# A fused attention, gating and mixing block on one core: where the first raw weights are loaded, and in what order batch 0's v projection uses them

## The chip, the cores and the metric

The kernel runs on one NeuronCore of one Trainium2 chip. The metric is the device time of one execution, in microseconds (us). Three runs of the kernel before took 501.28, 501.58 and 502.6 us; their median is 501.58 us.

The engines are named as in the profile: PE is TensorE (matmuls; PEld its weight loads), DVE VectorE, ACT ScalarE, POOL GpSimd, SP SyncE. SP, ACT and POOL also issue DMAs; SPq, ACTq and POOLq are these issues. Each engine runs its instructions in one fixed order, so an instruction that waits holds up all that stand behind it on that engine.

## The reference

Four batches of 576 tokens pass through three blocks. In outline:

```python
# attention: 8 heads of 64; heads 0-3 see the last 32 tokens, heads 4-7 every 32nd token
scores = q @ k.T / 8, masked;  attn = softmax(scores);  x = attn @ v          # x: 4 x 576 x 512
# gating block
h = relu(x @ w_in)                       # w_in 512 x 1024
u, v = h[..., :512], h[..., 512:]
v_n = (v - mean(v)) / sqrt(var(v) + 1e-6)
x = (u * (w_spatial @ v_n + b)) @ w_out
# mixing block
theta = x @ w_theta
y = w_tok_r @ (x * cos(theta)) + w_tok_i @ (x * sin(theta))
u = x + y;  out = u + relu(u @ w_ch)
```

Most weights arrive as 64-bit floats. The kernel loads their raw words and converts them on the chip into two 16-bit parts, "hi" and "lo"; a product is then three matmuls (hi by hi, lo by hi, hi by lo).

## The kernel before

`attention0` is batch 0's attention. It runs in steps s = 0 to 10 over eight groups of blocks (`quads0`): step s issues the scores of group s, the transposed outputs of group s-3, the transposed probabilities of group s-1 and the products with v of group s-2. While it runs, every engine keeps the order of the program (`pinned`). The dictionary `aside` hangs further work on the steps: the functions in the first list run in the middle of a step, those in the second at its end.

That further work is the input weight `w_in`. `win_piece(half, i, by)` gives five functions for one row block (128 rows by 512 columns) of one half: `[0]` the DMA of the raw words (512 KB), `[1:3]` two ACT passes over them, `[3]` a DVE pass that joins the two results, and `[4]` the split into the hi part (ACT) and the lo part (POOL). The half for v is `wv`, the half for u is `wu`; four row blocks each, numbered 0 to 3. The raw words of row blocks 0 and 1 lie in the buffer that the trace calls `x2f`, those of 2 and 3 in `zf`; the joined 32-bit numbers lie in `x2h`, the finished weights in `win`. `wu[i]` uses the same place as `wv[i]`, so its load waits until `wv[i][3]` has read the raw words. Later weights use the same two buffers: `w_spT` is loaded into `x2f` and `zf` next.

`main_v(0)` is batch 0's v projection, a generator that `go` moves on by one yield. It has five token tiles: pairs `pr` = 0 and 1 of two tiles of 128 tokens each, and a tail of 64 tokens. `v_mm(ps, tile, c)` adds the row block c of the weight to one tile with three matmuls of 512 columns. `v_relu` (ACT) empties a pair into `vr` and DVE takes mean and variance of it (BATCH_NORM_STATS2, then AGGREGATE); `norm` then makes `vn`. `main_mid(0)` goes on with `u_chunk(0..3)`, which need all four `wu`, and `sp_chunk(0..3)`, which need `vn` and `w_spT`. Both take their PSUM tile from a pool of three (`pm`) that the scores of batch 1 (`attention1`, tiles `a`) and the v projection use too.

After `attention0` the order is no longer pinned: `pinned.clear()` hands it to a scheduler, which works from the order of the program, from the time at which TensorE should be by its own count (`clock`), and from the list `conv` of due times of the remaining weights. In the traces of this kernel nearly every instruction has the line L107, that of the helper that issues it, so rows are told apart by their tiles.

Of the kernel before, what the change touches and what calls it, by code (L numbers as in the profile page):

```python
# [33 lines left out]
N32 = 3  # L34
# [23 lines left out]
PREP_AT = (112.0, 126.0, 131.0)  # L58
# [11 lines left out]
def kernel(  # L70
# [52 lines left out]
    nc = Engines  # L123
# [19 lines left out]
    NC = DM // P  # L143
# [76 lines left out]
    def s1(name):  # L220
        return scr.tile([P, S], F32, tag="s1", name=name, bufs=3)

    def pm(name):
        return ps_m.tile([P, 2, 512], F32, tag="pm", name=name)
# [67 lines left out]
    def win_piece(half, i, by):  # L292


        r = slice(i % 2 * DM, i % 2 * DM + DM)
        stg, x = (raw0, raw1)[i // 2][:, r], vals[i // 2][:, r]
        c = slice(half * DM, (half + 1) * DM)
        steps = from_f64(stg, x, DM)
        return [lambda: by.dma_start(stg, w_in[i * P:(i + 1) * P, c])] + steps + [
            lambda: part(win[:, 0, i:i + 1, c], win[:, 1, i:i + 1, c], x.unsqueeze(1), False)]  # L300
# [181 lines left out]
    def load_vs(b, v, hps, blocks=range(11), by=None):  # L482

        by = by or nc.sync
        src = vs_d[b].rearrange("h p n j d -> p h n (j d)")
        c = slice(1, VW - 1) if b == 0 else slice(0, P)
        hs = slice(hps[0] - 2, hps[-1] - 1)
        for i in blocks:
            k, end = CB * i, min(CB * i + CB, S)
            o = 0  # L490
            while k < end:
                n = max(range(5), key=lambda n: (SOFF[n] <= k) * (min(SOFF[n] + P, end) * 8 - n))
                m = min(end, SOFF[n] + P) - k
                p0 = k - SOFF[n]
                r = 64 * (i % 2) + o
                by.dma_start(v[r:r + m, :, i // 2, c], src[p0:p0 + m, hs, n])
                k += m
                o += m
# [29 lines left out]
    def load_mask16():  # L528
        mf = s1("mf")[:, 0:4 * P].rearrange("p (n c) -> p n c", n=4)
        nc.sync.dma_start(mf, mask_d)  # L530
        nc.gpsimd.tensor_copy(mask, mf)
# [114 lines left out]
    def attention0(aside):  # L646

        xf = xT[1].rearrange("p e c n -> p (e c n)").bitcast(F32)  # L650
        vf = wtok.rearrange("p e i n -> p (e i n)").bitcast(F32)
        qk = kts + [xf[:, i * 2 * S:(i + 1) * 2 * S].rearrange("p (j n) -> p j n", j=2) for i in range(2)]
        q, k = [t[:, 0] for t in qk], [t[:, 1] for t in qk]
        v01 = vf[:, 0:18 * VW].rearrange("p (h n d) -> p h n d", h=2, n=9)
        v23 = vf[:, 18 * VW:30 * VW].rearrange("p (h n d) -> p h n d", h=2, n=6)
        v = [v01[:, i] for i in range(2)] + [v23[:, i] for i in range(2)]
        S0, S1 = 2 * QB, 7 * CB + QB
        for hp in range(2):
            load_q(0, hp, q[hp], 0, S0, nc.sync)
            load_k(0, hp, k[hp], 0, S0, nc.scalar)  # L660
        for hp in (2, 3):
            load_qk(0, hp, q[hp], k[hp], 0, S1)
        nc.scalar.activation(x2f[:, 0, 0:1], halfpi, AF.Exp)
        for hp in (2, 3):
            load_k(0, hp, k[hp], S1, S, nc.scalar)
        make_masks()
        bias = bias_load()
        for n in range(2):
            nc.gpsimd.memset(v01[:, n, 0:9, 0:VW:VW - 1], 1.0)
            nc.gpsimd.memset(v23[:, n, 0:6, 0:VW:VW - 1], 1.0)  # L670
        load_vs(0, v23, (2, 3), range(8), nc.gpsimd)
        for f in aside[-1][:2]:
            f()
        load_vs(0, v23, (2, 3), range(8, 11), nc.gpsimd)
        for f in aside[-1][2:]:
            f()
        load_vl(0, v01, (0, 1), range(3))
        for hp in (2, 3):
            load_q(0, hp, q[hp], S1, S, nc.sync)
        for hp in range(2):  # L680
            load_qk(0, hp, q[hp], k[hp], S0, S)
        load_vl(0, v01, (0, 1), range(3, 4))
        load_mask16()
        un = {}
        for s in range(NG + 3):
            mid, end = aside.get(s, ((), ()))
            if s < NG:
                sc = pm("a0")
                t = s2("smx")
                sm, pT = t[:, 0, 0:512], t[:, 1, 0:512].rearrange("p (n k) -> p n k", n=4)  # L690
                st = att_p.tile([P, 2, 8], F32, tag="st", name="st", bufs=4)
                un[s] = sm, pT, st
                qd_scores(quads0[s], q, k, sc)
                qd_shift(quads0[s], sc, sm, st)
            if s >= 3:
                sm, pT, st = un.pop(s - 3)
                local = quads0[s - 3][0]
                qd_out(0, quads0[s - 3], pT, pm("xt")[:, 0, :] if local or s == 6 else pa("sc"))
            if 1 <= s <= NG:
                sm, pT, st = un[s - 1]  # L700
                qd_turn(quads0[s - 1], sm, pa4("av"), pT)
            if s < NG:
                qd_exp(quads0[s], un[s][0])
            if s == 1:
                bias_part(bias)
            for f in mid:
                f()
            if 2 <= s < NG + 2:
                sm, pT, st = un[s - 2]
                local = quads0[s - 2][0]  # L710
                qd_pv(quads0[s - 2], v, pT, pa("sc").unsqueeze(1) if local else pm("pv"), st, pT)
            for f in end:
                f()
# [277 lines left out]
    def main_v(b):  # L991
# [4 lines left out]
        def v_relu(pr, ps):  # L996
            v = vr[pr] = s2(f"vr{pr}")
            if pr == 2:
                fold_tail(v[0:TL, 0, 0:DM], v[0:TL, 1, 0:DM], ps[:, 0, :])
                ha.activation(v[0:TL, 0, 0:DM], v[0:TL, 0, 0:DM], AF.Relu, scale=1.0 / PS)  # L1000
                rows, nt = TL, 1
            else:
                ha.activation(v[:, :, 0:DM], ps, AF.Relu, scale=1.0 / PS)
                rows, nt = P, 2
            bs = att_p.tile([P, 2, 6], F32, tag="bs", name="bs")
            for t in range(nt):
                hv.bn_stats(bs[0:rows, t, :], v[0:rows, t, 0:DM])
                hv.bn_aggr(mv[0:rows, 2 * pr + t, :], bs[0:rows, t, :])
# [26 lines left out]
        def v_mm(ps, i, c):  # L1035
            for n, (xe, we) in enumerate(PASS):
                clock[0] += DM
                marks.append((clock[0] / 2400.0, nc.tensor.matmul(
                    ps, xh[:, xe, c, i * P:(i + 1) * P], win[:, we, c, DM:2 * DM],
                    start=(c == 0 and n == 0), stop=(c == NC - 1 and n == 2)).ins.name))  # L1040

        if b == 0:
            for pr in range(2):
                ps = pm(f"v{pr}")
                for ts, cs in (((range(2), (0, 1)), (range(2), (2, 3))), ((range(1), range(NC)), (range(1, 2), range(NC))))[pr]:
                    for c in cs:
                        for t in ts:
                            v_mm(ps[:, t, :], 2 * pr + t, c)
                    yield
                v_relu(pr, ps)  # L1050
                if pr == 0:
                    yield
            norm((0, 1))
        for pr in V_ORDER if b else V_ORDER[2:]:
            ps = pm(f"v{pr}")
# [174 lines left out]
    conv = []  # L1230
# [18 lines left out]
    timed(sq_parts(wch, w_ch, 2), *CONV_CH)  # L1249
    atts = [None] + [attention1(b) for b in range(1, N32)] + [attention(b) for b in range(N32, B)]  # L1250
    for at, f in [(at, lambda n=n: tok_load(*toks[n])) for n, at in enumerate(TOK_AT)] + [
            (at, lambda: next(atts[N32])) for at in PREP_AT]:
        i = next((i for i, c in enumerate(conv) if c[0] > at), len(conv))
        conv.insert(i, (at, f))
    att = {"b": 1, "n": 0}
# [26 lines left out]
    wt = pa("av")  # L1282
    for _ in range(WARM):
        nc.tensor.matmul(wt[:, 0:P], ident, ident, start=True, stop=True)
    wv, wu = ([win_piece(half, i, by) for i in range(NC)] for half, by in ((1, nc.gpsimd), (0, nc.sync)))
    v0 = main_v(0)

    def go():
# [1 line left out]

    attention0({
        -1: [w[0] for w in wv],
        3: ((), wv[0][1:3]),
        4: ((), wv[0][3:4] + wv[1][1:3] + wu[0][:1]),
        5: ((), wv[0][4:] + wv[1][3:4] + wv[2][1:3] + wu[1][:1]),
        6: ((), wv[1][4:] + wv[2][3:4] + wv[3][1:3] + wu[2][:1]),
        7: ((), wv[2][4:] + wv[3][3:4] + wu[3][:1] + [go, step]),
        8: ((), wv[3][4:] + wu[0][1:3] + [go]),
        9: ([go], wu[0][3:4] + wu[1][1:3] + [go]),
        10: ((), wu[0][4:] + wu[1][3:4] + wu[2][1:3] + [go]),  # L1300
    })
    conv[:0] = [(0.0, f) for f in wu[1][4:] + wu[2][3:] + wu[3][1:]]
    pinned.clear()
    run_main(v0)
    for b in range(B):
# [92 lines left out]
```

## Time and profile before

| | before |
|---|---|
| median of three runs | 501.58 us |
| the profiled execution | 499.96 us |
| its span on the core | 498.2 us |
| PE busy | 470.7 us (94%) |
| DVE busy | 301.5 us (61%) |
| ACT busy | 269.5 us (54%) |
| POOL busy | 83.1 us (17%) |

The span is the time between the first and the last instruction of the profiled execution; 1.76 us of the execution lie around it. PE is busy nearly all the time after the first 120 us, so what other engines do there matters only where PE waits for them. In the first 120 us PE does wait, and the profile has to be read stage by stage: which engine or transfer ends the wait. A row of the timeline gives start, duration, engine, operation, the tile written and the tiles read, and in brackets the idle time of that engine before it and what ended it.

### The profile page before, as it was taken

The numbers are of one execution on the slowest core, as the hardware profiler recorded it, in microseconds if no ns is written. First come the engines' busy times: TensorE is split into PE (matmuls) and PEld (weight loads), VectorE is DVE, ScalarE is ACT, GpSimd is POOL, SyncE is SP. The second block draws the span as 40 slices with busy tenths as digits, with TensorE's granted clock in tenths as the row PEclk, the third lists the DMA queues.
The fourth block names the chain that finished last, engine by engine and source line by source line (L and its number), as shares of the span: only waits on it lengthen the run. The fifth ranks groups of instructions, "written<-read, shape, count | busy, mean of one in ns | idle before, by whom it ended". The sixth has DMA issues, their size and how long they took to land. (4 is left out here: it accounts for less than half of the span.)

```text
span 498.2 us, 10844 instructions
## 1 busy us (share of the span) xinstructions
PE 470.7 (94%) x4446; PEld 352.6 (71%) x4446; DVE 301.5 (61%) x653; ACT 269.5 (54%) x488; POOL 83.1 (17%) x86
## 2 busy tenths in 40 slices
PE   7578789889999999999999999999999999999996
PEld 5354466667667777777658777777657777777775
DVE  3465799886798744763488677872588121217412
ACT  3347678878984433545763767764862022148302
POOL 9313304320001500111001310021004200210220
PEclk9999999999999999999999999999999999999999
DMA  7937766664891035210174155321170020004502
GB/s 175 280 99 202 191 225 201 214 221 135 210 216 37 2 130 180 68 44 2 25 172 150 23 138 170 76 43 22 31 160 2 1 95 1 1 2 67 125 0 97
DMA packets 72250, 52.73 MB, mean 106 GB/s; under 512 B 51198, under 2 KB 61008, under 8 KB 72200
## 3 DMA queue, kind: packets, MB, share of 16 engines
q1 hardware_dynamic: 70248, 49.03, 36.5%
q0 software_dynamic: 1312, 2.70, 2.0%
q8 instruction: 35, 0.57, 0.5%
q10 hardware_dynamic: 640, 0.30, 0.3%
q14 instruction: 15, 0.12, 0.1%
HBM read 35.36 MB, written 4.72 MB: 80 GB/s over the span
## 5 line engine op out<-in xcount | busy, mean ns | idle before, releaser
L107 PE MATMUL y<-wtok,zf 128*128 128x288 f16 x864 | 107.2, 286 | 0.0
L107 PEld LDWEIGHTS <-zf 128*128 128x128 f16 x864 | 84.1, 98 | 22.2 <-issue 1.2
L107 PE MATMUL u<-xT,win 128*128 128x288 f16 x384 | 49.3, 286 | 2.3 <-ACT u L107 2.0
L107 PE MATMUL sp<-wsp,vn 128*128 128x288 f16 x384 | 50.5, 286 | 0.0
L107 POOL TENSOR_TENSOR x2h<-x2f,x2h 128x576 f16<-128x576 f32 x19 | 26.2, 1384 | 142.2 <-issue 66.7
L107 PE MATMUL x<-zf,wout 128*128 128x288 f16 x384 | 49.6, 286 | 0.0
L107 PE MATMUL v<-win,xT 128*128 128x512 f16 (+1 forms) x240 | 48.3, 380 | 0.0
L107 PE MATMUL th<-x2h,wth 128*128 128x288 f16 x384 | 47.7, 286 | 0.0
L107 PEld LDWEIGHTS <-vn 128*128 128x128 f16 x416 | 40.3, 98 | 10.2 <-DVE vn L107 0.5
L107 PEld LDWEIGHTS <-win 128*128 128x128 f16 x384 | 37.3, 98 | 11.8 <-issue 2.7
L107 PE MATMUL c<-x2h,wch 128*128 128x288 f16 x360 | 45.2, 286 | 0.0
L107 PEld LDWEIGHTS <-wth 128*128 128x128 f16 x384 | 37.6, 98 | 9.5
L107 PEld LDWEIGHTS <-wch 128*128 128x128 f16 x384 | 37.4, 98 | 9.2
L107 PEld LDWEIGHTS <-wout 128*128 128x128 f16 x384 | 36.8, 98 | 9.5
L107 PEld LDWEIGHTS <-xT 128*128 128x128 f16 (+1 forms) x240 | 21.0, 100 | 24.7 <-issue 1.3
L107 ACT ACTIVATE x2h<-x2f 128x576 f16<-128x576 f32 (+2 forms) x30 | 21.3, 709 | 24.9 <-DVE x2f L107 23.5
L107 POOL TENSOR_TENSOR zf<-u,zf 128x576 f16<-128x576 f32 x8 | 10.3, 1282 | 112.9 <-ACT zf L107 112.9
L107 ACT ACTIVATE o<-c 128x576 f32<-128x576 f32 x15 | 9.7, 646 | 34.9 <-PE c L107 34.7
L107 DVE TENSOR_TENSOR ta<-ta,x2f 128x1152 f32<-128x1152 f32 (+1 forms) x17 | 21.7, 1283 | 11.2 <-ACT ta L107 11.2
L107 DVE SCALAR_TENSOR_TENSOR x2f<-y,x2f 128x576 f32<-128x576 f32 x16 | 12.0, 752 | 24.6 <-PE y L107 24.5
L107 DVE SCALAR_TENSOR_TENSOR o<-x2f,o 128x576 f32<-128x576 f32 (+1 forms) x17 | 12.2, 722 | 23.7 <-ACT o L107 23.7
L107 DVE TENSOR_TENSOR u<-u,sp 128x576 f32<-128x576 f32 x16 | 12.0, 750 | 22.1 <-PE sp L107 22.1
(145 smaller groups left out, 743.3 us busy)
## 6 DMA issues: line engine op xcount, KB each, us to landing
out_dram<-o SPq DMA_DIRECT2D x15, 288.0 KB
kt<-in_qp_dram SPq DMA_DIRECT2D x8, 288.0 KB
qs<-in_qd_dram SPq DMA_DIRECT2D x8, 288.0 KB
xT<-in_w_ch_dram SPq DMA_DIRECT2D x2, 1024.0 KB
kt<-in_kzl_dram SPq DMA_DIRECT2D x8, 152.0 KB
ks<-in_kl_dram SPq DMA_DIRECT2D x4, 304.0 KB
v<-in_vl_dram SPq DMA_DIRECT2D x8, 144.0 KB
kt<-in_kzs_dram SPq DMA_DIRECT2D x8, 144.0 KB
```

What stands on the lines that cost most here:

```text
L107: ins = f(*args, **kwargs)
```

## The change

All of it concerns batch 0.

- The raw loads of `wv` are issued by SP instead of POOL, behind all loads of batch 0's q, k and v. Before, POOL issued them, the first two between two groups of its own loads of v, the others behind these.
- The load of the mask that only the last batch uses, and its cast on POOL, move from the start into the list `conv`, with the time 15.0.
- Each part of the conversion of `wv` moves to a later step: the first ACT passes of `wv[0]` run at the end of step 4 instead of step 3, and so on. The conversions of `wu` keep their steps or move, and those left over at the end of `attention0` run at once, still in the pinned order, instead of standing first in `conv`.
- The v projection goes weight row block by row block. Before: row blocks 0 and 1, then 2 and 3 for the first pair of tiles; then all four for tile 2 and all four for tile 3. Now: row block 0 for tiles 0 and 1 (step 7); row block 1 for tiles 0 and 1 and row blocks 0 and 1 for tile 2 (step 8); row block 2 for tiles 0, 1 and 2, and row blocks 0, 1, 2 for tile 3 (step 9); row block 3 for all four tiles, with the two `v_relu` (step 10). Both PSUM tiles are open from step 8 to step 10.

```diff
@@ attention0
-        load_vs(0, v23, (2, 3), range(8), nc.gpsimd)
-        for f in aside[-1][:2]:
-            f()
-        load_vs(0, v23, (2, 3), range(8, 11), nc.gpsimd)
-        for f in aside[-1][2:]:
-            f()
+        load_vs(0, v23, (2, 3), range(11), nc.gpsimd)
...
         load_vl(0, v01, (0, 1), range(3, 4))
-        load_mask16()
+        for f in aside[-1]:
+            f()
@@ main_v
         if b == 0:
-            for pr in range(2):
-                ps = pm(f"v{pr}")
-                for ts, cs in (((range(2), (0, 1)), (range(2), (2, 3))), ((range(1), range(NC)), (range(1, 2), range(NC))))[pr]:
-                    for c in cs:
-                        for t in ts:
-                            v_mm(ps[:, t, :], 2 * pr + t, c)
-                    yield
-                v_relu(pr, ps)
-                if pr == 0:
-                    yield
+            ps = []
+
+            def some(pr, cs, ts=(0, 1)):
+                for c in cs:
+                    for t in ts:
+                        v_mm(ps[pr][:, t, :], 2 * pr + t, c)
+
+            ps.append(pm("v0"))
+            some(0, (0,))
+            yield
+            some(0, (1,))
+            ps.append(pm("v1"))
+            some(1, (0, 1), (0,))
+            yield
+            some(0, (2,))
+            some(1, (2,), (0,))
+            some(1, (0, 1, 2), (1,))
+            yield
+            for pr in range(2):
+                some(pr, (3,))
+                v_relu(pr, ps[pr])
+            yield
             norm((0, 1))
@@ the list of due times
-            (at, lambda: next(atts[N32])) for at in PREP_AT]:
+            (at, lambda: next(atts[N32])) for at in PREP_AT] + [(15.0, load_mask16)]:
@@ the steps
-    wv, wu = ([win_piece(half, i, by) for i in range(NC)] for half, by in ((1, nc.gpsimd), (0, nc.sync)))
+    wv, wu = ([win_piece(half, i, by) for i in range(NC)] for half, by in ((1, nc.sync), (0, nc.sync)))
...
-        3: ((), wv[0][1:3]),
-        4: ((), wv[0][3:4] + wv[1][1:3] + wu[0][:1]),
-        5: ((), wv[0][4:] + wv[1][3:4] + wv[2][1:3] + wu[1][:1]),
-        6: ((), wv[1][4:] + wv[2][3:4] + wv[3][1:3] + wu[2][:1]),
-        7: ((), wv[2][4:] + wv[3][3:4] + wu[3][:1] + [go, step]),
-        8: ((), wv[3][4:] + wu[0][1:3] + [go]),
-        9: ([go], wu[0][3:4] + wu[1][1:3] + [go]),
-        10: ((), wu[0][4:] + wu[1][3:4] + wu[2][1:3] + [go]),
+        4: ((), wv[0][1:3]),
+        5: ((), wv[0][3:4] + wv[1][1:3] + wu[0][:1]),
+        6: ((), wv[0][4:] + wv[1][3:4] + wv[2][1:3] + wu[1][:1]),
+        7: ((), wv[1][4:] + wv[2][3:4] + wv[3][1:3] + wu[2][:1] + [go, step]),
+        8: ((), wv[2][4:] + wv[3][3:4] + wu[3][:1] + wu[0][1:3] + [go]),
+        9: ((), wv[3][4:] + wu[0][3:4] + wu[1][1:3] + [go]),
+        10: ((), [go] + wu[0][4:] + wu[1][3:4] + wu[2][1:3]),
     })
-    conv[:0] = [(0.0, f) for f in wu[1][4:] + wu[2][3:] + wu[3][1:]]
+    for f in wu[1][4:] + wu[2][3:] + wu[3][1:]:
+        f()
```

On SP, around the last loads of batch 0's q, k and v (`kt` holds q and k, `wtok` holds v for now, `mf` is the mask, `x2f` and `zf` are the raw weight buffers), the order before was:

```order
L107 DMA kt_81<-in_kzl_dram 64x448 x2
L107 DMA wtok<-in_vl_dram 96x3x128 x2
L107 DMA mf<-in_mask_dram 128x512
L107 DMA x2f<-in_w_in_dram 128x512 x2
L107 DMA zf<-in_w_in_dram 128x512 x2
L107 DMA kt_80<-in_qp_dram 128x576
```

and it is now:

```order
L107 DMA kt_81<-in_kzl_dram 64x448 x2
L107 DMA wtok<-in_vl_dram 96x3x128 x2
L107 DMA x2f<-in_w_in_dram 128x512 x2
L107 DMA zf<-in_w_in_dram 128x512 x2
L107 DMA x2f<-in_w_in_dram 128x512 x2
L107 DMA zf<-in_w_in_dram 128x512
L107 DMA kt_80<-in_qp_dram 128x576
```

The first four `w_in` loads of the second list are those of `wv`, which stood on POOL; those of `wu` follow, the last of them now behind batch 1's first loads. The mask's load is gone from here.

On ACT, from the end of the v projection to the first `u` (`vr` is the relu of v, `win<-x2h` the hi part of a row block, `x2f<-x2f` with `x2h<-x2f`, and `zf<-zf` with `x2h<-zf`, the two passes over raw words, `wsp` the spatial weight), the order before was:

```order
L107 ACTIVATE vr_594<-v_531 128x2x512
L107 ACTIVATE x2f<-x2f 128x512
L107 ACTIVATE x2h<-x2f 128x512
L107 ACTIVATE win<-x2h 128x512
L107 ACTIVATE xT_94<-xt 128x2x64
L107 ACTIVATE win<-x2h 128x512
L107 ACTIVATE zf<-zf 128x512
L107 ACTIVATE x2h<-zf 128x512
L107 ACTIVATE win<-x2h 128x512
L107 ACTIVATE vr_646<-v_612 128x2x512
L107 ACTIVATE win<-x2h 128x512
L107 ACTIVATE vr_764<-v_673 64x512
```

and it is now:

```order
L107 ACTIVATE vr_638<-v_572 128x2x512
L107 ACTIVATE win<-x2h 128x512
L107 ACTIVATE zf<-zf 128x512
L107 ACTIVATE vr_761<-v_680 64x512
L107 ACTIVATE x2h<-zf 128x512
L107 ACTIVATE vr_761<-vr_761 64x512
L107 ACTIVATE win<-x2h 128x512 x2
L107 ACTIVATE zf<-zf 128x512
L107 ACTIVATE x2h<-zf 128x512
L107 ACTIVATE sm<-sm 128x384
L107 ACTIVATE wsp<-x2f 128x1152
L107 ACTIVATE win<-x2h 128x512
```

All four hi parts of `wu` now stand behind both large relus of v, and the last of them also behind the first pass over `w_spT` (`wsp`); before, three of them stood ahead of the second large relu (`vr_646`), and all four ahead of `wsp`.

## Rows read from the trace of the kernel before

**Rows 1.** Busy time by stage: start:end, length, per engine, PEclk, DMA share, GB/s

```profile
19.80:27.35 7.55, 2.71 (x29) 1.63 (x24) 1.06 (x3) 1.28 (x3) 0.00 (x0) 1.00 1.02 276
27.35:40.57 13.22, 9.69 (x165) 7.47 (x163) 10.80 (x28) 9.05 (x20) 2.83 (x3) 1.00 0.25 85
40.57:56.30 15.73, 14.12 (x99) 6.79 (x99) 8.75 (x23) 11.47 (x24) 6.04 (x6) 1.00 0.84 205
56.30:78.00 21.70, 18.72 (x211) 13.56 (x212) 20.17 (x63) 15.43 (x22) 2.14 (x3) 1.00 0.65 194
78.00:118.55 40.55, 36.29 (x465) 27.64 (x464) 32.34 (x63) 32.71 (x54) 12.21 (x10) 1.00 0.61 208
118.55:498.20 379.65, 373.53 (x3316) 283.86 (x3313) 219.09 (x451) 192.62 (x359) 44.31 (x31) 1.00 0.31 78
```

**Rows 2.** PE's waits up to 118.55 us: total, times, longest

```profile
PE a L107 <- DMA kt<-in_kzl_dram: 6.1, 5, 3.2
```

**Rows 3.** Page, part 2: GB/s in 40 slices of 12.45 us

```profile
GB/s 175 280 99 202 191 225 201 214 221 135 210 216 37 2 130 180 68 44 2 25 172 150 23 138 170 76 43 22 31 160 2 1 95 1 1 2 67 125 0 97
```

**Rows 4.** DMA issues: KB each, median us from issue to landing

```profile
zf<-in_w_in_dram POOLq DMA_DIRECT2D x2, 512.0 KB, 10.5
```

**Rows 5.** Timeline, 12 to 32 us

```profile
12.34 1.14 POOL L107 DMA_DIRECT2D x2f<-in_w_in_dram  x2
...
14.53 1.26 SPq L107 DMA_DIRECT2D kt<-in_kzl_dram  x2
...
19.80 0.53 PE L107 MATMUL a<-kt 64*64 64x96 f32 x4
...
25.19 0.59 PE L107 MATMUL a<-kt 64*64 64x96 f32 x4 [3.22 <-DMA kt<-in_kzl_dram]
...
26.85 0.50 PE L107 MATMUL a<-mask,identb 128*128 128x192 bf16 x2
...
29.91 0.86 PE L107 MATMUL a<-kt 64*64 64x96 f32 x16
...
31.25 0.68 DVE L107 SCALAR_TENSOR_TENSOR x2h<-x2f,x2h 128x512 int32<-128x512 int32 x1
```

**Rows 6.** Timeline, 34 to 53 us

```profile
34.76 1.17 DVE L107 SCALAR_TENSOR_TENSOR x2h<-x2f,x2h 128x512 int32<-128x512 int32 x1
...
40.57 2.76 PE L107 MATMUL v<-win,xT 128*128 128x512 f16 x12
...
48.53 1.00 ACT L107 ACTIVATE vr<-v 128x1024 f32<-128x1024 f32 x1
...
49.57 0.69 DVE L107 BATCH_NORM_STATS2 bs<-vr 128x6 f32<-128x512 f32 x1
...
50.40 0.66 DVE L107 BATCH_NORM_STATS2 bs<-vr 128x6 f32<-128x512 f32 x1
...
52.12 4.17 PE L107 MATMUL v<-win,xT 128*128 128x512 f16 x24
```

**Rows 7.** Timeline, 53 to 78 us

```profile
53.80 0.40 SPq L107 DMA_DIRECT2D x2f<-in_w_spT_dram  x1
...
54.63 0.62 ACT L107 ACTIVATE win<-x2h 128x512 f16<-128x512 f32 x1
...
55.32 1.16 POOL L107 TENSOR_TENSOR win<-x2h,win 128x512 f16<-128x512 f32 x1 [0.48 <-ACT win L107]
...
56.99 0.56 PE L107 MATMUL a<-kt 64*64 64x96 f32 x16
...
57.81 1.16 ACT L107 ACTIVATE wsp<-x2f 128x1152 f16<-128x1152 f32 x1 [0.52 <-DMA x2f<-in_w_spT_dram]
...
58.17 3.10 PE L107 MATMUL u<-xT,win 128*128 128x288 f16 x24 [0.35 <-DVE vr L107]
...
63.25 3.10 PE L107 MATMUL u<-xT,win 128*128 128x288 f16 x24 [1.98 <-ACT u L107]
...
77.44 0.41 PE L107 MATMUL sp<-wspt,k 128*128 128x288 f16 x2
```

## Prediction

> **What bounds the kernel now.** I read the busy time by stage first. From 118.55 us to the end PE is busy 373.53 of 379.65 us: PE sets the time there, the change removes none of its work, and I leave those 379.65 us as they are [rows 1]. So the question is only how early PE gets to 118.55. Before that the stages differ. From 19.80 to 27.35 PE is busy 2.71 of 7.55 us, DVE 1.06, ACT 1.28, while the DMA engines are busy the whole time (share 1.02) at 276 GB/s [rows 1]: a transfer is the limit. From 27.35 to 40.57 DVE has 10.80 of 13.22; from 40.57 to 56.30 PE has 14.12 of 15.73; from 56.30 to 78.00 DVE has 20.17 of 21.70 and is the bound; from 78.00 on PE leads with 36.29 of 40.55, DVE and ACT behind it with some 32.5 each [rows 1].
>
> PE's waits name the transfer: 6.1 us for `kt<-in_kzl_dram`, the rest of k of the local heads [rows 2]. The timeline shows the first in place: group 4's scores begin at 19.80 and their mask ends at 26.85+0.50 = 27.35, with a wait of 3.22 in one piece [rows 5]. SP had issued the last of this k by 14.53+1.26 = 15.79; POOL had put `wv`'s first raw loads beside it from 12.34 [rows 5].
>
> **The change, part by part.**
>
> *The loads.* The two slices up to 24.9 us moved 12.45 x (175+280) = 5.66 MB [rows 3], of which `wv` is 4 x 512 KB = 2.10 MB. Without it 3.56 MB are left; 2.18 of them went in the first slice, and 1.38 MB at 280 GB/s take 4.9 us: there at 17.4 by bandwidth. By issue: 15.79 plus at most the 4.0 us that a load five times as large took from issue to use (53.80 to 57.81 [rows 7]) is 19.8. Either way group 4 need not wait. Its 16 matmuls then cost 0.86 and the mask 0.50, as rows of that stretch do [rows 5]: it ends at 19.80+1.36 = 21.2 instead of 27.35, **6.2 us earlier**. `wv` follows on SP's queue, 2.10 MB at 280 GB/s = 7.5 us, so its pieces land from about 20 to 27; the first is now wanted at the end of step 4, about 24, one more per step. Hidden, by 2 us or more; each us that a piece came later would cost one.
>
> SP issues these loads now. The mask's place and four issues of 0.4 to 0.6 us (`w_spT`'s took 0.40 [rows 7]) end before 20 us; the next on SP is `wu[0]`, which waits for the DVE pass of `wv[0]` at about 27. Nothing queues behind them. The Trainium skill ("DMA: Bandwidth & Descriptors", "Issuing engines are not separate DMA queues") says that issuing from several engines saves only the issue time, since all transfers run on the same 16 DMA engines; by that the move itself gives no bandwidth and costs SP the issues. The slices cannot separate the two, and the sum does not use it.
>
> *Conversions a step later.* The DVE pass of 0.68 at 31.25 goes from step 4's end [rows 5], and the slow one at 34.76, 1.17, a step later has an ordinary one, 0.68, in its place [rows 6]. DVE is the bound there, so about 1.2 us: v starts at 40.57-6.2-1.2 = **33.2**. Row block 0 is the only one needed then.
>
> PE's rate: 16 score matmuls take 0.86 at 29.91 [rows 5] and 0.56 at 56.99 [rows 7], so the durations are those of the lower clock (1.2 GHz) at first, although the granted-clock column reads 1.00 [rows 1]. With no gap from 20 to 25 the rise to 2.4 GHz can come earlier. It is worth 0 to 1 us, since DVE takes over as the limit; I take 0.
>
> *v by row blocks.* PE does the same 48 matmuls and the tail, but the first relu comes after 42 of them: 42 x 0.23 (2.76/12 [rows 6]) = 9.7, and for the attention's own matmuls between them 1.7 (PE's 14.12 in that stage [rows 1] less 36 x 0.23 and 4.17 [rows 6]) with 0.5 allowed for hand-overs: 33.2+11.9 = **45.1**, against 48.53 [rows 6]: only 3.4 earlier. The last pair and the tail end at 45.1+1.4+1.5 = 48, against 52.12+4.17 = 56.29 [rows 6].
>
> *`wu` behind v.* Here PE waits anew. First relu 45.1 to 46.1, then on DVE four statistics at 0.83 each (49.57 to 50.40 [rows 6]) to 49.4, the tail's sum about 0.6 (an estimate by the 512-column passes), and `wu[1]`'s pass 0.68: 50.7. Only now is `x2f` free for `w_spT`; its load takes 4.0 (53.80 to 57.81 [rows 7]): 54.7. `wsp` on ACT 1.16, the last hi part 0.62, its lo part on POOL 1.16 [rows 7]: 57.7. So `u0`, started near 50, ends at about 58.0, against 58.17+3.10 = 61.27: **3.3 earlier**. PE stands idle for some 6 us in this stretch; that is where the 8.3 us at the end of v go. But the next chunk need no longer wait the 1.98 us for ACT's `u`, which stood behind `wsp` from `zf`: it starts at 58.0 against 63.25 [rows 7], **5.2 earlier**.
>
> *Norm and `sp`.* DVE bounds 56.3 to 78. Its statistics start 3.4 earlier, and about 2.5 us of its work now stands behind the norm in its order (an estimate by 0.68 for 512 columns [rows 5]: 1.3 for a 1024-column pass of `w_out`, as much for small ones of batch 1's softmax): `sp0` ends 5.9 earlier than 77.85 [rows 7]. These 2.5 us come due between 78 and 118.55, where DVE has 32.34 of 40.55 [rows 1]; I charge a quarter, 0.6, against the smaller of the two shifts: 5.2-0.6 = **4.6 us**.
>
> *Sum.* 499.96-4.6 = 495.4 for the profiled execution (span 498.2, 1.76 around it). The median of the runs, 501.58, lies 1.62 above; the prediction is for a median: **497.0**. Bounds: a gain of 8.3 (all of v's shift) and, with rival 4, a loss of 4.3.
>
> **Rivals.**
>
> 1. *More gets through* (chance 0.12): the rate rises early, and the loads for `wu` and `w_spT` find free DMA engines (share 0.25 from 27.35 to 40.57 [rows 1]). Against: ACT's order has `wsp` ahead of the last hi part whatever the load does. Gain about 7: 494.6.
>
> 2. *DVE and ACT give it back* (0.13): the work deferred past `sp0` delays batch 1's softmax, and PE's transposes wait for it. For it: DVE and ACT are at 80% from 78 to 118.55 [rows 1]. Against: PE has 4.26 us of idle time there too. With the whole 2.5 charged the gain is 5.2-2.5 = 2.7: 498.9.
>
> 3. *Hidden anyway* (0.10): `kzl` is early, but `wv` lands late and v's use of the weights stays where it was. For it: one such load took 10.5 us from issue [rows 4]; four in a row from 17 us on may need until 30. Against: those shared the engines with all of q, k and v. Gain under 1.5: 501.
>
> 4. *Slower* (0.10): one mechanism, the load of `w_spT` ahead of `wu`'s last hi part on ACT. If it takes the 10.5 us of [rows 4] instead of 4.0, `u0` ends at 64.5 and the next chunk starts 1.2 us later than before; it decides from a load of 9.3 us on. PE, nearly idle for 12 us by then, is also likely to be at the lower clock, and the next chunk's 3.10 [rows 7] become 6.2: 501.58+1.2+3.1 = 505.9. Against: the load took 4.0 before, at a share of 0.84 [rows 1].
>
> 5. *Lower clock alone* (0.05): the load is in time, but the thin stretch from 50 to 58 sends PE back to 1.2 GHz and the next chunk takes 3.1 more: gain 1.5, 500.1. Against: after the wait of 1.98 us before it the 24 matmuls at 63.25 take 3.10, as those at 58.17 do [rows 7]; nothing after 31 us shows the lower rate. The Trainium skill ("TensorE: Matmul & The Clock Gate", "HAM oscillation — how this bites in real kernels") says that waits for DMA between bursts of matmuls put the array back to the lower clock, so that each burst starts slow. The trace of before has no such case past 31 us.
>
> **How the numbers follow.** The forecast, a gain of 3 to 6.2, has 0.50. The range for 8 in 10 goes from 493.5, which holds most of rival 1, to 501.5, which holds 2, 3 and 5 and leaves out 4. Differences within 0.3%, 1.5 us, can't be told from none. Faster by more: 0.50+0.12 and the 0.13 of rival 2, 0.75; within: rivals 3 and 5 less a little for worse cases, 0.14; slower: rival 4 and these, 0.11.
>
> **What would show it.** Group 4's scores without a `kzl` wait, mask done by 22; v's first matmul at 32 to 35; first `vr` near 45; `u0` in pieces between 50 and 58, waiting for `win`; `w_spT` on ACT about 4 us after its issue; the next chunk at 58; the stage that began at 118.55 beginning near 114 and lasting 379 to 380. Wrong would be: v later than 37; `u0` ending after 61; new waits of PE between 78 and 118 that sum to over 3 us; a longer last stage.

## The result and the profile after

The changed kernel takes 504.58 us (median of 19 runs, 502.64 to 508.07). Beside it the kernel before took 502.4 us (19 runs, 500.63 to 505.36). The ratio is 1.0055, with a 95% interval of 1.0035 to 1.0075: slower by 0.55%, some 2.8 us (2.2 by the medians), where a gain of 4.6 was forecast. The profiled execution took 503.2 us with a span of 501.4, against 499.96 and 498.2.

The windows of the profile after, cut at the same stages; th, the matmuls with w_th, now begins at 114.28 instead of 118.55. Columns as in [rows 1].

```profile
19.80:27.35 7.55, 5.38 (x125) 4.18 (x119) 6.09 (x17) 4.97 (x11) 0.00 (x0) 1.00 0.88 284
27.35:40.57 13.22, 11.23 (x104) 6.68 (x105) 8.73 (x25) 9.14 (x22) 3.80 (x3) 0.87 0.59 171
40.57:56.30 15.73, 13.20 (x99) 6.71 (x98) 11.60 (x32) 9.84 (x17) 5.09 (x4) 0.91 0.73 167
56.30:78.00 21.70, 19.52 (x202) 14.11 (x201) 21.13 (x53) 15.84 (x25) 4.97 (x4) 0.99 0.59 193
78.00:114.28 36.28, 31.59 (x387) 23.82 (x385) 29.49 (x50) 27.15 (x42) 12.86 (x10) 1.00 0.70 229
114.28:501.40 387.12, 376.71 (x3348) 285.41 (x3345) 220.01 (x457) 195.80 (x364) 44.29 (x31) 0.99 0.29 76
```

Up to th the times came out close to the forecast: th starts 4.27 us earlier. The last stage, left as it was in the sum, is 387.12 us instead of 379.65 [rows 1], 7.47 longer, and PE is not busy for 10.41 us of it instead of 6.12. The span grew by 7.47 - 4.27 = 3.2.

The first half, on the timeline of the profile after (start, duration, engine, instruction; in brackets the idle time before it and what ended it):

```profile
20.84 0.62 PE L107 MATMUL a<-kt 64*64 64x96 f32 x8 [0.95 <-DMA kt<-in_kzl_dram]
21.39 0.34 PE L107 MATMUL a<-mask,identb 128*128 128x192 bf16 x2
...
31.62 0.41 PE L107 MATMUL xt<-ident,smx 128*128 128x128 f32 x2 [1.89 <-DVE smx L107]
...
33.10 2.74 PE L107 MATMUL v<-win,xT 128*128 128x512 f16 x6
...
45.90 1.02 ACT L107 ACTIVATE vr<-v 128x1024 f32<-128x1024 f32 x1 [1.02 <-PE v L107]
...
53.94 5.33 PE L107 MATMUL u<-xT,win 128*128 128x288 f16 x31 [1.31 <-POOL win L107]
...
56.01 1.15 ACT L107 ACTIVATE wsp<-x2f 128x1152 f16<-128x1152 f32 x1
...
60.18 1.28 PE L107 MATMUL u<-xT,win 128*128 128x288 f16 x9 [0.91 <-POOL win L107]
...
71.25 0.41 PE L107 MATMUL sp<-wspt,k 128*128 128x288 f16 x2
```

Group 4's mask ends at 21.73 instead of 27.35 [rows 5], v starts at 33.10 instead of 40.57, the first relu at 45.90 instead of 48.53 [rows 6], and the sp0 tail stands at 71.25 instead of 77.44 [rows 7]: 6.2 earlier.

Now the place where it was lost: PE around th, before and then after.

```profile
115.60 3.11 PE L107 MATMUL x<-zf,wout 128*128 128x288 f16 x24
118.55 11.92 PE L107 MATMUL th<-x2h,wth 128*128 128x288 f16 x96
130.31 11.94 PE L107 MATMUL v<-win,xT 128*128 128x512 f16 x60
```

```profile
114.28 0.53 PE L107 MATMUL th<-x2h,wth 128*128 128x288 f16 x3
114.75 0.67 PE L107 MATMUL av<-pT,v 54*64 54x54 f32 x16
115.35 0.54 PE L107 MATMUL th<-x2h,wth 128*128 128x288 f16 x3
115.82 0.67 PE L107 MATMUL sc<-pT,v 54*64 54x54 f32 x16
116.43 8.26 PE L107 MATMUL th<-x2h,wth 128*128 128x288 f16 x66
128.53 4.71 PE L107 MATMUL th<-x2h,wth 128*128 128x288 f16 x24 [3.85 <-DVE ta L107]
133.07 11.94 PE L107 MATMUL v<-win,xT 128*128 128x512 f16 x60
```

th has four parts of 24 matmuls each, in PSUM tiles from the pool of three, so the fourth part can start only when the first has been emptied. Before, the 96 matmuls ran in one piece. After, batch 1's last two groups of products (av and sc from pT; they ended at 115.6 before) stand inside th, about 1.2 us; PE waits 3.85 us; and the 24 matmuls behind the wait take 4.71 instead of 24/96 of 11.92 = 2.98, so 1.73 more. From the start of th to batch 1's v are 18.79 us instead of 11.76: 7.03 more, of which these three make 6.8. Less the 4.27 gained, batch 1's v starts 2.76 later than before: that is most of the 3.2 by which the span grew. From there to the end the two executions take nearly the same, 367.89 and 368.33.

Who frees the PSUM tile for the fourth part? ACT's rows with DVE's row of `ta<-th`, before and then after, there with SP's issue of the last `w_ti` load:

```profile
124.12 0.75 ACT L107 ACTIVATE xT<-xT 128x576 f32<-128x576 f32 x1 [0.63 <-DMA xT<-in_w_ti_dram]
...
125.39 1.17 ACT L107 ACTIVATE ta<-th 128x576 int32<-128x576 f32 x2
126.19 1.42 DVE L107 SCALAR_TENSOR_TENSOR ta<-th,ta 128x576 f32<-128x576 f32 x2
126.45 1.16 ACT L107 ACTIVATE wtok<-wx 128x1152 f16<-128x1152 f32 x1
```

```profile
116.82 1.23 ACT L107 ACTIVATE xT<-xT 128x1152 f32<-128x1152 f32 x1
...
120.61 0.33 SPq L107 DMA_DIRECT2D xT<-in_w_ti_dram  x1
...
124.58 0.72 ACT L107 ACTIVATE xT<-xT 128x576 f32<-128x576 f32 x1 [1.64 <-DMA xT<-in_w_ti_dram]
125.21 1.15 ACT L107 ACTIVATE wtok<-wx 128x1152 f16<-128x1152 f32 x1
...
126.87 1.71 ACT L107 ACTIVATE ta<-th 128x576 int32<-128x576 f32 x3
127.73 2.08 DVE L107 SCALAR_TENSOR_TENSOR ta<-th,ta 128x576 f32<-128x576 f32 x3
```

`ta<-th` on ACT reads the finished parts of th, and DVE's `ta<-th` frees the PSUM tile behind it: after, the first of the three on DVE ends near 128.4, and PE goes on at 128.53. In ACT's queue it stands behind the last piece of the token weights (`tok_step`), which starts when its load is in, at 124.58; before it was 124.12. So this load and all that hangs on it stayed near their old time while PE came 4.3 us earlier, and `wtok<-wx` has slipped in front. The load goes out only when the third piece's passes have freed its buffer (120.61; 120.10 before), and these stand on ACT behind the emptying of batch 1's last attention groups. Before, there was little to spare: DVE freed the first PSUM tile at about 126.9, and PE came for it at about 127.5 (estimates, half of 1.42 after 126.19 and three quarters of 11.92 after 118.55). The Trainium skill ("PSUM — Partial Sum Buffer", "Engine vs sequencer instructions") says that ScalarE's queue is strict first in, first out. The trace agrees: the finished parts lie ready while ACT idles 1.64 us for a load that they don't need.

### The profile page after: what moved, and what is told of

Same layout as the page of the kernel before. It is cut to its first block, busy times and chain, and to the rows that moved or that the text cites. A ratio compares the mean times of both kernels' runs of the same rounds, so it can differ in the third digit from the quotient of the medians.

```text
span 501.4 us, 10837 instructions
## 1 busy us (share of the span) xinstructions
PE 472.3 (94%) x4446; PEld 351.8 (70%) x4446; DVE 306.3 (61%) x653; ACT 269.6 (54%) x488; POOL 84.3 (17%) x82
## 5 line engine op out<-in xcount | busy, mean ns | idle before, releaser
L107 PE MATMUL u<-xT,win 128*128 128x288 f16 x384 | 50.9, 291 | 3.4 <-POOL win L107 2.2
L107 PE MATMUL th<-x2h,wth 128*128 128x288 f16 x384 | 49.8, 292 | 3.8 <-DVE ta L107 3.8
L107 PE MATMUL v<-win,xT 128*128 128x512 f16 (+1 forms) x240 | 49.5, 386 | 0.0
```

The costliest lines, as they stand in the source:

```text
L107: ins = f(*args, **kwargs)
```

## Experiments

The ratio is to the kernel before on the same chip. Runs of one kernel spread by some 1%, so each variant was run 6 to 12 times, and pairs (the same edit on both kernels) are compared by their ratios. "Worth" is the changed kernel's ratio over the other's; its interval joins the two half widths as the root of their squares.

### Is it the queue on ACT?

In the changed kernel the token weights' steps are shifted as a whole, their last due at 54 us of TensorE work and not at 50 (e1); the same in the kernel before (e2); or only the last step is put behind th's emptying (e5).

```
-CONV_TOK = (61.0, 11.0, 4.0)          # e1, e2
+CONV_TOK = (61.0, 7.0, 4.0)
-    timed([lambda n=n: tok_step(n) for n in range(len(toks))], *CONV_TOK)    # e5
+    for n, at in enumerate((34, 38, 42, 46, 53.5)):
+        conv.append((at, lambda n=n: tok_step(n)))
```

> The changed kernel, with one number different: the lead of the token weights' conversions is 7 instead of 11, so that on ACT the last piece (w_ti's tail, whose load is late) stands behind the emptying of the first two th tiles instead of ahead of it. Theory A (the loss of the changed kernel is this queue on ACT: PE waits 3.85 us in th for a PSUM tile and then runs about 1.8 us slower): the wait falls under 0.5 us and the 24 matmuls after it take 3 instead of 4.7, so some 5 us less than the changed kernel, 499 to 500, 0.5% below before. Theory B (ACT and DVE are behind with the work put off past sp0, and the wait only moves): a new wait of 2 us or more in th or at the start of y, 502 to 504.5. Theory C (PE's lower clock in several gaps costs the time, not the wait): 503 or more.

> The kernel before with the same number, 7 instead of 11, alone. Theory A: before had no such wait in th (th ran 11.92 us in one piece), so no change, within 0.3% of 502.4. If it is faster by more than 0.3%, the lead is a gain of its own and e1 says less about the change.

> The changed kernel with only the last piece of the token weights moved: due at 53.5 on the kernel's own count, so that it stands on ACT right behind the emptying of the first two th tiles, and on DVE ahead of batch 1's statistics (in e1 it stood behind them, and y waited 6.8 us). Theory A (the queue on ACT is the loss): th's wait falls from 3.85 to under 1 us, y waits under 0.5 us, the 24 matmuls take 3 us, the whole 500 to 501. Theory B (the chain of the token weights itself is late, wherever it stands): a wait of 2 us or more in th or y remains, 503 to 506.

Measured: e1 509.53 us, 1.0118 (1.0086 to 1.0151); e2 507.45, 1.0071 (1.0044 to 1.0099); e5 505.69, 1.0051 (1.0021 to 1.0081). The wait in th did go, and came back elsewhere. PE in e5, where only 0.55 us of the 3.85 are left and v waits instead:

```profile
127.40 3.10 PE L107 MATMUL th<-x2h,wth 128*128 128x288 f16 x24 [0.55 <-DVE ta L107]
...
138.76 8.03 PE L107 MATMUL v<-win,xT 128*128 128x512 f16 x36 [3.08 <-DVE ta L107]
```

And PE in e1, where the waits stand between y's first matmul and the next batch, 6.84 us in four:

```profile
143.08 6.78 PE L107 MATMUL y<-wtok,zf 128*128 128x288 f16 x54 [1.26 <-ACT vr L107]
150.71 15.60 PE L107 MATMUL y<-wtok,zf 128*128 128x288 f16 x126 [0.85 <-DVE x2f L107]
...
172.54 0.56 PE L107 MATMUL a<-kt 64*64 64x96 f32 x16 [1.06 <-DVE x2f L107]
...
177.05 0.94 PE L107 MATMUL av<-ident,sm 128*96 128x128 f32 x4 [3.67 <-DVE sm L107]
```

So the place in the queue is only where the shortage shows. My first theory, that this order on ACT is the loss, fell: it wanted 499 to 500 of e1 and 500 to 501 of e5. e1 came out slower than theory B's 502 to 504.5 too; theory C's 503 or more has it, but without C's reason, since the 24 matmuls behind the wait take 3.10 in e1 and e5 (4.71 in the changed kernel). What is short is time on ACT and DVE: work put off later is waited for later. e2 missed as well: no change was expected, and the kernel before lost 0.7%, with 3.7 us of such waits in its trace (0.80, 1.19 and 1.72). So the shift costs either kernel, and with it the change is worth 1.0047 (1.000 to 1.009), much as without it.

### Which part of the change matters?

e3 gives `wv`'s loads back to GpSimd; e4 puts `wu`'s last pieces back into the list of conversions.

```
-    wv, wu = (... ((1, nc.sync), (0, nc.sync)))        # e3
+    wv, wu = (... ((1, nc.gpsimd), (0, nc.sync)))
-    for f in wu[1][4:] + wu[2][3:] + wu[3][1:]:        # e4
-        f()
+    conv[:0] = [(0.0, f) for f in wu[1][4:] + wu[2][3:] + wu[3][1:]]
```

> The changed kernel with the loads of wv issued by POOL again, behind its loads of v; all else as changed. If the early arrival of kzl comes from the loads' place on SP, the wait of group 4's scores comes back (some 4 to 5 us between 20 and 26 us), v starts at 37 or later instead of 33.1, and th starts some 3 to 4 us later than in the changed kernel. Theory A then lets the wait in th shrink by as much, since the late load there is not moved by PE's earlier arrival: the whole kernel stays within 1.5 us of the changed one, though v is 4 us later. Theory B and C: slower than the changed kernel by 2 to 4 us.

> The changed kernel with the remaining steps of wu left to the scheduler again (first in the list of due times) instead of run in the pinned order. By the prediction's chain u0 then no longer has the last hi part behind wsp: the first two u chunks, which end at 61.5 in the changed kernel, end 1 to 3 us earlier and PE's waits for win (2.2 us on POOL's lo part) shrink. Theory A: no gain at the end, since what PE gains before th is waited for in th: within 1 us of 504.6. Theory B: 1 to 3 us faster.

Measured: e3 510.53, 1.0119 (1.0079 to 1.0158); e4 503.81, 1.0007 (0.9985 to 1.003). PE, POOL and ACT in e3:

```profile
14.82 1.14 POOL L107 DMA_DIRECT2D x2f<-in_w_in_dram  x2 [0.53 <-issue]
...
23.41 0.58 PE L107 MATMUL a<-kt 64*64 64x96 f32 x4 [2.97 <-DMA kt<-in_kzl_dram]
...
132.01 0.71 ACT L107 ACTIVATE xT<-xT 128x576 f32<-128x576 f32 x1 [1.68 <-DMA xT<-in_w_ti_dram]
...
135.95 4.40 PE L107 MATMUL th<-x2h,wth 128*128 128x288 f16 x24 [3.88 <-DVE ta L107]
```

From GpSimd the first raw loads go out at 14.82, before SP has issued all of q, k and v, and the wait for `kzl` is back with 2.97 us; the changed kernel issues them on SP at 18.39. Going out behind q, k and v, as they do on SP, is what gives the early start. Theory A, which wanted e3 within 1.5 us of the changed kernel, fell here too: e3 is 0.6% slower by the ratios, 3.2 us, in theory B's and C's 2 to 4 (5.9 by the medians). The wait in th is 3.88 us in this execution as well, though it ends 7.4 us later. ACT again stands before a `w_ti` load, and this load is later by as much, 132.01 for 124.58: it is no fixed time that PE runs into, the load hangs on the order of the work ahead of it.

e4 is faster than the changed kernel: the two intervals do not touch, and e4 over the changed kernel is 0.995 (0.992 to 0.998), some 2.4 us, in theory B's 1 to 3 (by the medians only 0.8). With `wu`'s last pieces left to the scheduler no difference to before is left. By this pair some 2.4 of the 2.8 us lost hang on running these pieces in the pinned order. In its profiled execution batch 1's products are out of th, and the wait there is 2.73 us.

### Is it the clock?

e8 adds ten matmuls whose result is not used, 2.47 us in its trace, ahead of v, where PE waits 1.89 us.

```
+                if s == 7:
+                    for _ in range(10):
+                        nc.tensor.matmul(xt[:, 0:P], ident, ident, start=True, stop=True)
```

> The changed kernel with ten more matmuls of the identity, whose result is overwritten, in step 7, where PE waits about 1.9 us for DVE (29.8 to 31.6) and where the first six v matmuls then took 2.74 instead of 1.38 us. Theory C (the lower clock after such gaps costs the time): those six take about 1.4, v ends 1 to 2 us earlier, the whole 1 to 2 us below 504.6. Theories A and B: v ends earlier by as much, but the wait in th takes it back: within 0.5 us of 504.6.

Measured: 507.27 us, 1.0079 (1.0049 to 1.011). PE in e8:

```profile
32.96 1.47 PE L107 MATMUL v<-win,xT 128*128 128x512 f16 x6
...
69.67 0.41 PE L107 MATMUL sp<-wspt,k 128*128 128x288 f16 x2
...
114.13 0.53 PE L107 MATMUL th<-x2h,wth 128*128 128x288 f16 x3
...
128.55 4.65 PE L107 MATMUL th<-x2h,wth 128*128 128x288 f16 x24 [4.02 <-DVE ta L107]
```

The first six matmuls of v take 1.47 instead of 2.74 and the sp0 tail comes 1.6 us earlier, but th starts only 0.15 earlier (114.13 for 114.28). Most of the gain is gone ahead of th, between 78 and 114, where one wait for DVE has grown from 1.02 to 2.45 us; the wait in th is then 4.02 and ends at 128.55, as it did at 128.53. What PE gains early is not seen behind th. Theory C, which wanted a gain of 1 to 2 us, fell. The time itself lies 2.7 us above the 504.6 that theories A and B wanted within 0.5; the ratio, 1.0079, can't be told from the changed kernel's 1.0055. In th the lower clock is 1.73 us of the loss, behind the wait and as its consequence. Nor do the kernels differ in it: the mean granted clock of 35 runs of before is 0.979, of 19 runs of the changed kernel 0.983.

### Is it the token weights' work?

Their steps due earlier, in both kernels (e6, e7) and with e4's edit (e11); then their passes on ACT and DVE left out in both (e9), with zeros written by GpSimd.

```
+    for n, at in enumerate((33, 36.5, 40, 44, 50)):    # e6, e7, e11; before: 34, 38, 42, 46, 50
+        conv.append((at, lambda n=n: tok_step(n)))
-        tok_part(*toks[n])                             # e9
+        i, m = toks[n][0], min(2, NZ - toks[n][0])
+        nc.gpsimd.memset(wtok[:, :, i:i + m, :], 0.0)
```

> The changed kernel with the third and fourth piece of the token weights earlier (due 40 and 44 instead of 42 and 46): on ACT the third piece then stands ahead of the emptying of batch 1's last attention groups, so its buffer is free about 4 us sooner and the load of the last piece is issued near 116 instead of 120.6. Theory B says that this late load is the cause: th's wait falls to under 1 us, y does not wait, the whole 499 to 501. Theory A, taken alone (the order on ACT, unchanged here at that place), says that the wait goes only as far as the load is earlier: the same. Theory C (lower clock): under 1 us better than 504.6.

> The kernel before with the same earlier third and fourth piece, the control for e6. Before has no wait in th, so within 0.3% of before by theories A and B; a gain over 0.3% would be one of the pieces themselves.

> The kernel before with the conversion of the token weights left out (their five loads stay; GpSimd fills the tiles with zeros in place of the ACT and DVE passes, so the output is wrong by the token layer's product; nothing else is changed). It is the base for the next run. Expected by every theory: near the time of before or up to 3 us under it (500 to 503), since in before the passes over the token weights stand beside a TensorE that waits for none of them between 118.5 and 142 us. More than 4 us faster would say that this chain bounds before too.

> The changed kernel with the same left out. What counts is its difference to the run above. If the token weights' passes on ACT and DVE are what holds th's emptying and with it swallows the gain (queue or backlog alike): 3 to 4.5 us faster than the run above, the 4.3 us by which th starts earlier, and no wait over 1 us in th. If the rest of the ACT and DVE work (attention of batch 1, conversions of w_out and w_th) is late as well: 0 to 2 us faster, with a wait of 2 us or more in x or th. If the lower clock in the gaps is the loss: still 1 to 3 us slower than the run above.

> The changed kernel with two edits that each helped a little: the last pieces of wu go through the list of conversions again (as before the change), and the token weights' steps are due at 33, 36.5, 40, 44 and 50 instead of 34, 38, 42, 46 and 50. If the chain of the token weights is what is late, the edits add: 500.5 to 502.5, 0.3 to 0.8% under the changed kernel and 0 to 0.4% under before. If the ACT and DVE work as a whole is the bound, the earlier steps only push other work back: 503 to 505.

Measured: e6 502.57, 0.9979 (0.9954 to 1.0005); e7 503.47, 1.0019 (0.999 to 1.0049); e11 500.73, 0.9959 (0.9936 to 0.9982). Without the passes: before 500.79, 0.9967 (0.9937 to 0.9997); changed 500.05, 0.994 (0.9908 to 0.9971). e6 missed its 499 to 501: the load went out at 119.04 and not near 116; the wait in th did fall to 0.62, as theories A and B have it, but from th to batch 1's v it is still 18.43 us, since more of batch 1's attention now stands inside th. e7, the control, stayed within its 0.3%. e11 hit the 500.5 to 502.5 of the reading that the two edits add; e4's part alone is not clear of noise in it (e11 over e6 is 0.998).

PE in the two profiled executions of e9, first the kernel before without the passes, then the changed one without them:

```profile
119.65 11.92 PE L107 MATMUL th<-x2h,wth 128*128 128x288 f16 x96
131.41 11.94 PE L107 MATMUL v<-win,xT 128*128 128x512 f16 x60
```

```profile
115.62 11.92 PE L107 MATMUL th<-x2h,wth 128*128 128x288 f16 x96
127.38 11.94 PE L107 MATMUL v<-win,xT 128*128 128x512 f16 x60
```

With the passes gone, th runs in one piece and the 4.03 us that it starts earlier reach batch 1's v whole. That is what the theory of the backlog expects, in the traces; 2.8 of it are left at the end of the span. The runs do not bear it out to the same size: the change is then worth 0.997 (0.993 to 1.002), some 1.4 us (0.7 by the medians), and not 3 to 4.5. That is the size of the second reading, 0 to 2, but the wait of 2 us or more in x or th that belongs to it is not in the trace. Against the 1.0055 with the passes that is clear of noise, against nothing it is not. So the token weights are part of the loss; that they are all of it is not shown.

### Is it batch 1's attention?

Its steps are due every 4.2 us of TensorE work. With 3.9 in the changed kernel (e12) and in before (e17); with 3.9 and the earlier token weights in both (e13, e15); with e4's edit as well (e14); with 3.7 (e18).

```
-ATT_AT = (None, (2.7, 4.2), (86.0, 5.4), (174.5, 4.6))
+ATT_AT = (None, (2.7, 3.9), (86.0, 5.4), (174.5, 4.6))
```

> The changed kernel with the token weights' steps as in the run above (wu as in the changed kernel) and batch 1's attention spaced by 3.9 us of TensorE work instead of 4.2, so that its last two groups of products stand in x and no longer in th. If the late attention of batch 1 is what delays the emptying of th on ACT: 499.5 to 502, th in one piece with under 1 us of waiting. If ACT and DVE have no slack in the stages sp and x: TensorE waits there for the softmax instead (idle in sp and x up by 2 to 4 us), and the time is 503 to 506.

> The changed kernel with one edit: batch 1's attention spaced by 3.9 us of TensorE work instead of 4.2 (the token weights' steps stay where they are). It takes apart the two edits of the run above that gave 499.5. If the late attention in ACT's and DVE's order alone delays the emptying of th: 500 to 502. If the token weights' due times alone count: 503.5 to 505, as the changed kernel. Half of each, 502 to 503, if the two are one backlog on ACT.

> The changed kernel with all three edits: wu's last pieces in the list of conversions, the token weights' steps due at 33, 36.5, 40, 44 and 50, and batch 1's attention spaced by 3.9 us. If the backlog around th is the only loss: 497 to 499.5, the 4 us by which th starts earlier reach the end. If ACT and DVE are full between 57 and 118 us: no better than two of the edits, 499.5 to 501.5.

> The kernel before with the same new spacing of batch 1's attention (3.9 us) and the same due times of the token weights' steps. It tells what the change itself is worth once both are spaced alike. If the backlog of ACT and DVE at th, which only the changed kernel meets, is what swallows the gain: 502 to 505, no faster than before, so that the change is worth 3 us or more with this spacing. If the spacing alone is the gain, with or without the change: 499 to 501.

> The kernel before with one edit, batch 1's attention spaced by 3.9 us instead of 4.2: the partner of the changed kernel with the same edit (500.84 us). If the spacing is the key that the changed kernel lacked: 502.5 to 505, so the change is worth 2 to 4 us with it. If the spacing alone brings the gain: 500 to 501.5.

> The changed kernel with the token weights' steps due at 33, 36.5, 40, 44 and 50 and batch 1's attention spaced by 3.7 us, one step beyond the fastest variant (3.9 us, 499.49). If there is still slack on ACT and DVE between 57 and 118 us: 497.5 to 499. If it is used up at 3.9: 500 to 503, with TensorE waiting for the softmax in u and sp.

Measured:

| edit | kernel before | changed kernel | the change is worth |
|---|---|---|---|
| none | 502.4 | 504.58, 1.0055 | 1.0055 (1.0035 to 1.0075) |
| attention 3.9 | 507.26, 1.0072 (1.0043 to 1.0101) | 500.84, 0.9943 (0.9917 to 0.997) | 0.987 (0.983 to 0.991) |
| 3.9, tokens early | 505.23, 1.0023 (1.0 to 1.0046) | 499.49, 0.9929 (0.9901 to 0.9957) | 0.991 (0.987 to 0.994) |
| tokens early | 503.47, 1.0019 | 502.57, 0.9979 | 0.996 (0.992 to 1.000) |

The changed kernel's e12 and e13 came out as the reading of late attention has it. e14 gave 501.49, 0.9967 (0.9942 to 0.9993), and e18 501.09, 0.996 (0.9933 to 0.9987), both in the reading of no slack left: no more was gained by the third edit or a closer spacing. The 3.9 does not help the kernel before, it costs it 3.6 us, more than e17 expected; the changed kernel gains 3.7 by the medians, 5.6 by the ratios. With it the change is worth 6.4 us, and 4.7 with the tokens early as well. That 4.7 lies near the 4.6 forecast confirms nothing: 3.6 of the 6.4 and 1.2 of the 4.7 are what the same due times cost the kernel before. Against the kernel before as it was, the changed kernel with the best due times tried (e13) gains 0.7%, 3.6 us; it is the lowest of several variants, which flatters it.

PE and ACT in e12:

```profile
73.60 0.61 PE L107 MATMUL av<-ident,sm 128*96 128x128 f32 x4 [1.37 <-DVE sm L107]
...
114.71 1.26 ACT L107 ACTIVATE xT<-xT 128x1152 f32<-128x1152 f32 x1
...
119.35 11.92 PE L107 MATMUL th<-x2h,wth 128*128 128x288 f16 x96
...
124.69 0.65 ACT L107 ACTIVATE ta<-th 128x576 int32<-128x576 f32 x1 [0.16 <-PE th L107]
125.24 1.16 ACT L107 ACTIVATE wtok<-wx 128x1152 f16<-128x1152 f32 x1
...
131.11 11.94 PE L107 MATMUL v<-win,xT 128*128 128x512 f16 x60
```

The products are out of th, the token pass at 114.71 comes 2.1 us earlier on ACT than in the changed kernel (116.82), `ta<-th` waits for PE and for nothing else, and th runs in one piece. PE pays with new waits earlier, as at 73.60; th starts 5 us later than in the changed kernel (1.8 of it are there at v already, which the edit does not touch), and batch 1's v still 1.96 earlier. The kernel before had no wait in th to lose, and it pays as well: from u's first matmul to sp's last it takes 45.75 us in e17 and 45.33 in e15, against 41.20 to 44.53 in its four profiled executions with the old spacing (before, e2, e7, e9). That this is all of the 3.6 us is not shown. The fastest, e13, is 0.7% faster than before and some 1.2% faster than the changed kernel.

## Why the prediction was wrong

- *Loads, conversions, v.* Right: v at 33.10 for 33.2, first relu at 45.90 for 45.1. That the order of issue made `kzl` late is shown by e3. That the number fits so well is luck: in the ten other profiled executions with the same order up to v, it starts between 33.51 and 35.98 (and between 40.47 and 43.05 in the five variants of before).
- *`wu` behind v.* Right in its mechanism, `u` in pieces that wait for `win`, `wsp` at 56.01, 4.4 us after its load was issued at 51.56. The first two chunks of u, 48 matmuls, end at 61.46 for a forecast of 58.0 + 3.10 = 61.1 (66.35 before [rows 7]); 1.3 us of this is the lower clock in the 31 matmuls at 53.94 (5.33 us for about 4.0).
- *sp0 5.9 earlier, th 4.6 earlier.* Right: 6.2 and 4.27.
- *The last stage left as it is.* This step failed. "PE sets the time there, the change removes none of its work" was read from a busy share of 373.53 of 379.65 us [rows 1]. That share says PE did not wait for ACT and DVE when it came at 118.55. It does not say by how much. On the timeline of before `ta<-th` on ACT came at 125.39, behind a load waited for until 124.12, and the PSUM tile was free about 0.6 us before PE wanted it: slack was near none. PE came 4.3 us earlier, ACT's and DVE's work for batch 1 and the token weights did not, and the stage grew by 7.47. Up to batch 1's v PE lost 3.85 by waiting, 1.73 by slower matmuls and 1.2 to batch 1's products, which came inside th. The prediction itself had named a longer last stage as a sign of being wrong.
- *The rivals.* Rival 2 named the right engines and charged at most 2.5 us, between 78 and 118.55. There it was right: of the 6.2 at sp0's tail 1.9 were given back by th. The sum charged 0.6 and came out 0.3 off only because it started from the smaller shift, 5.2. The larger bill came behind the line at which the sum stopped. Rival 4, the slower one, did not occur: the load took 4.4 us at most. Rival 5 put the lower clock behind a thin stretch at 50 to 58; it was there, and worth 1.3 us.
- *The reference execution.* The sum started from an execution at a granted clock of 1.000; the 35 later runs of before had 0.959 to 0.999, and all of them took longer than its 499.96 us. The loss in th does not hang on this: from th's start to batch 1's v it is 11.76 us in e2 and e17 too, variants of before, and 18.52 and 18.91 in e3 and e8, variants of the changed kernel.

Shown: the emptying of th waits on ACT and DVE, the wait moves with the order of their work, it is gone from the changed kernel when a part of that work is left out, and with batch 1's attention spaced by 3.9 the change is worth 6.4 us against a kernel before that loses 3.6 by the spacing. Not settled: how the loss divides between the token weights, the attention and the pinned order of `wu`'s last pieces, since e9's traces and medians differ in size and e4's gain does not add to that of the others (e14 is no faster than e13).

## What to carry to other kernels

A stage in which one engine is busy all the time is not safe from being reached earlier: before a gain is carried through it, look at its first hand-overs and ask when the other engines would be ready, and for each buffer that comes free there by how much it is early. Where other work is placed by due times written against one engine's progress, a change that moves that engine makes these numbers wrong; time it again with them shifted, and give the kernel before the same shift, or the comparison measures the tuning. If the shift harms the kernel before, compare also each at its own best.

## What the runs showed of the hardware

- A wait can cost twice, once as a wait and once in the matmuls behind it: the 24 matmuls behind 3.85 us of waiting took 4.71 us instead of 2.98, and the first six of v 2.74 behind thin work and 1.89 us of waiting, 1.47 with the gap filled. Against the same matmuls at 2.4 GHz that is 1.58 and 1.86 times as long, so more than half of the one burst and nearly all of the other ran at 1.2 GHz; the window from 114.28 to 133.07 shows a granted clock of 0.91. The Trainium skill ("TensorE: Matmul & The Clock Gate", "HAM oscillation — how this bites in real kernels") tells this of waits for DMA; the trace has it for an ACT and DVE wait as well. Not every wait did it: behind 1.98 us before [rows 7] the 24 matmuls took 3.10.
- The mean granted clock of one program, the kernel before, varied from 0.959 to 0.999 over 35 runs, and its time from 500.22 to 506.98 us.
- Edits of a few due times moved the median of the changed kernel between 499.5 and 509.5 us, and that of the kernel before between 502.4 and 507.5, as much as any part of the change.
